# Opening: rests of k from ScalarE's queue and an earlier gate for GpSimd's loads; ending: a bank of its own for the last product and three queues for its stores

## The chip, the cores and the metric

One core of a Trainium2 chip. The metric is the device time of one execution in microseconds (us). "Fast" is the normal state of the runs; every comparison here is within that state, and every profile shown is of a fast run. The profiled span (from the first record to the last) is some 1.8 us shorter than the device time of the same run.

## The reference

A linear attention (phi(x) = elu(x) + 1) over 8 batches, 8 heads, 576 positions of 64, then a mixture of four dense experts:

```python
def phi(x): return np.where(x > 0, x, np.exp(x) - 1.0) + 1.0
kv  = np.einsum('bhsd,bhse->bhde', phi(k), v);  z = np.sum(phi(k), axis=2)
num = np.einsum('bhsd,bhde->bhse', phi(q), kv)
x   = num / (np.einsum('bhsd,bhd->bhs', phi(q), z)[..., None] + 1e-6)   # -> 4608 x 512
p   = domain_probs / (domain_probs.sum(-1, keepdims=True) + 1e-9)
for e in range(4):
    out += p[:, e:e+1] * (np.maximum(x @ w1[e], 0.0) @ w2[e])           # 512 -> 1024 -> 512
```

## The kernel before

The 576 positions of a batch are cut into 512 "first" ones and a "rest" of 64. A list of operations is ordered by a planner in the program: each operation has an engine, an estimated duration and a priority; GpSimd's order is the order in which the program adds its operations. Each layer's matrix product is done in seven half-size block products in place of eight. Four things matter here.

Loads. Every load is a DMA issued by a named queue. `hold` makes it wait for the landing of the load that carries the same `mark`:

```python
def load_first(queue, pri, t, pr, hold=None, mark=None):      # 256 KB: two heads, 512 positions
    ...
def load_first_rest(t, o, queue, pri, key, g):                # 32 KB: two heads, 64 positions
    n = 2 * R // DC
    dma(queue, pri, o[g * n : (g + 1) * n].rearrange("p h t d -> p h (t d)"),
        t[0, 2 * g : 2 * g + 2, NT:S].rearrange("h (p t) d -> p h (t d)", t=2),
        ((key, g),), 0.17)
```

The order of the first loads ("pair" is a pair of heads, counted from 0 to 3):

```python
load_first("SP", -9, k, 0, mark="k0")
load_first("SP", -8, q, 0)
load_first("SP", -7, k, 1)
for g in range(DC):
    load_first_rest(k, k_r, "ACT" if g < 2 else "SP", -6, "k_r", g)
for g in range(DC):
    load_first_rest(v, v_r32, "SP", -4, "v_r32", g)
load_first("SP", -3, q, 1)
load_first("POOL", 0, v, 0, hold="k0")          # GpSimd starts when k of pair 0 is in
for pr in (2, 3):
    load_first("POOL", 0, k, pr)
    load_first("POOL", 0, q, pr)
    if pr == 2:
        load_first("POOL", 0, v, 1)
        load_w1(0, (0,))                        # first quarter of the first w1, 128 x 1024
load_first("POOL", 0, v, 2)                     # eighth load of GpSimd
load_first("POOL", 0, v, 3)
```

The last products. P1 to P7 are the block products of layer two; a product is four matmuls into half of one of four PSUM banks:

```python
P4 = (2, 1, ...)        # bank 2, upper half
P3 = (2, 0, ...)        # bank 2, lower half: the last one
seq = (P1, P6, P5, P7, P4, P2, P3)              # in the very last unit
```

The six final adds on VectorE, and the four last stores (64 x 512 each, 128 KB):

```python
for dur, o, a_, b_, r, w in (
    (0.4,  of[:, 0],   hi(1), s15[:, 0], ...),
    (0.4,  of[:, 1],   hi(0), of[:, 0], ...),
    (0.62, of[:, 2:4], lo(3)[:, None].broadcast_to([P, 2, HD]), of[:, 0:2], ...),   # third
    (0.4,  of[:, 2],   hi(2), of[:, 2], ...),                                       # fourth
    (0.4,  of[:, 0],   lo(1), s15[:, 0], ...),
    (0.4,  of[:, 1],   lo(2), of[:, 1], ...),
):
    ...
    if i in (3, 5):
        for par, queue in enumerate(("SP", "ACT")):
            store(int(i == 3), par, queue, (O(2 if i == 3 else 0),))
```

Of the kernel before, what the change touches and what calls it, by code (L numbers as in the profile page):

```python
# [137 lines left out]
def kernel(  # L138
# [23 lines left out]
    HF = FC // 2  # L162
# [167 lines left out]
        dma(queue, pri, o, t[0, 2 * pr : 2 * pr + 2, 0:NT].rearrange("h (p c) d -> p h c d", c=C),  # L330
            (key,), 0.72, hold=hold, mark=mark)

    def load_first_rest(t, o, queue, pri, key, g):

        n = 2 * R // DC
        dma(queue, pri, o[g * n : (g + 1) * n].rearrange("p h t d -> p h (t d)"),
            t[0, 2 * g : 2 * g + 2, NT:S].rearrange("h (p t) d -> p h (t d)", t=2),
            ((key, g),), 0.17)

    def load_rest(b, queue, pri, after=0.0, parts=(0, 1, 2)):  # L340
        par = b % 2
# [636 lines left out]
    def l2_unit(n):  # L978
        j, s, e = units[n]
        h, s4 = h_b[n % 2], s4_b[n % 2]  # L980
        first, last = e == 0, e == E - 1
        H = lambda t, f: ("h", n % 2, t, f)
        Q = lambda i: ("s4", n % 2, i)
        KW = lambda i, j_: k2(e, i, j_)
        T = lambda i: (("t", e, i),)

        def prod(bank, half, a, w, opens):
            for c in range(HF):
                nc.tensor.matmul(  # L989
                    out=l2b[bank][:, half * HD : (half + 1) * HD],  # L990
                    lhsT=a[:, c, :],
                    rhs=w[:, c],
                    start=(opens and first and c == 0),
                    stop=(last and c == HF - 1),
                    skip_group_check=True,
                )

        P2 = (1, 0, h[:, 0, 1], H(0, 1), quad(e, 1, 0), KW(1, 0), True)
        P4 = (2, 1, h[:, 1, 1], H(1, 1), quad(e, 0, 1), KW(0, 1), True)
        P1 = (0, 0, h[:, 0, 0], H(0, 0), quad(e, 0, 0), KW(0, 0), True)  # L1000
        P5 = (0, 1, s4[:, 0], Q(0), t123[e][:, 0], T(0), False)
        P6 = (1, 1, s4[:, 1], Q(1), t123[e][:, 1], T(1), False)
        P7 = (3, 0, s4[:, 2], Q(2), t123[e][:, 2], T(2), True)
        P3 = (2, 0, s4[:, 3], Q(3), quad(e, 1, 1), KW(1, 1), False)
        seq = (P1, P4, P5, P2, P6, P7, P3)
        end = n == nu - 1
        if first:
            seq = (P1, P5, P2, P6, P7, P4, P3)
        elif end:
            seq = (P1, P6, P5, P7, P4, P2, P3)  # L1010
        p0 = U(n + 1) + 0.45
        for i, (bank, half, a, ak, w, wk, opens) in enumerate(seq):
            pl.add("PE", 0.436, p0 + 0.9 * i,
                   lambda bank=bank, half=half, a=a, w=w, opens=opens: prod(bank, half, a, w, opens),
                   r=(ak,) + wk, w=lk(bank) + ((("p", bank, half),) if end else ()))
        if not last:
            return
        oi = rot("ot", 2)
        ot = ot_b[oi]
        of = ot.rearrange("p a (b d) -> p (a b) d", b=2)  # L1020
        O = lambda i: ("ot", oi, i // 2)
        tt = nc.vector.tensor_tensor
        v2 = lambda bank: bank.rearrange("p (a d) -> p a d", a=2)
        s1, s5 = (s15[:, i : i + 1].broadcast_to([P, 2, HD]) for i in range(2))
        sk = ("s15", "ident", ("kvz", 2), ("kvz", 3))
        if end:
            pl.add("ACT", 0.36, p0, lambda: nc.scalar.copy(s15[:, 0], l2b[0][:, 0:HD]),
                   r=(("p", 0, 0),), w=sk)
        else:
            pl.add("ACT", 0.5, p0 + 3.5, lambda: nc.scalar.copy(  # L1030
                s15.rearrange("p a d -> p (a d)"), l2b[0]), r=("l2b0",), w=sk)
        stores = [(u, par) for u in range(2) for par in range(2)]

        def store(u, par, queue, r):
            b = 2 * (2 * s + u) + par
            dma(queue, p0 + 9, out[b * S + NT : (b + 1) * S, :],
                ot[par * R : (par + 1) * R, u, :], (), 0.3, r=r)

        if end:
            lo, hi = (lambda bank: l2b[bank][:, 0:HD]), (lambda bank: l2b[bank][:, HD : 2 * HD])  # L1040
            for dur, o, a_, b_, r, w in (
                (0.4, of[:, 0], hi(1), s15[:, 0], (("p", 1, 1), "s15"), (O(0),)),
                (0.4, of[:, 1], hi(0), of[:, 0], (("p", 0, 1),), (O(0),)),
                (0.62, of[:, 2:4], lo(3)[:, None].broadcast_to([P, 2, HD]), of[:, 0:2],
                 (("p", 3, 0), O(0)), (O(2),)),
                (0.4, of[:, 2], hi(2), of[:, 2], (("p", 2, 1),), (O(2),)),
                (0.4, of[:, 0], lo(1), s15[:, 0], ("l2b1",), (O(0),)),
                (0.4, of[:, 1], lo(2), of[:, 1], lk(2), (O(0),)),
            ):
                i = cnt.get("lp", 0)  # L1050
                cnt["lp"] = i + 1
                pl.add("DVE", dur, p0 + 2 + i * 0.5,
                       lambda o=o, a_=a_, b_=b_: tt(out=o, in0=a_, in1=b_, op=AO.add), r=r, w=w)  # L1053
                if i in (3, 5):
                    for par, queue in enumerate(("SP", "ACT")):
                        store(int(i == 3), par, queue, (O(2 if i == 3 else 0),))
            return
        pl.add("DVE", 0.62, p0 + 4.5, lambda: tt(
            out=of[:, 0:2], in0=v2(l2b[1]), in1=s1, op=AO.add), r=("l2b1", "s15"), w=(O(0),))
        pl.add("DVE", 0.4, p0 + 5.5, lambda: tt(  # L1060
            out=of[:, 2], in0=l2b[3][:, 0:HD], in1=of[:, 1], op=AO.add),
            r=("l2b3", O(0)), w=(O(2),))
        pl.add("DVE", 0.62, p0 + 6.5, lambda: tt(
            out=of[:, 1:4:2], in0=of[:, 1:3], in1=s5, op=AO.add), r=("s15",), w=(O(0), O(2)))
        pl.add("DVE", 0.62, p0 + 8, lambda: tt(
            out=of[:, 1:3], in0=v2(l2b[2]), in1=of[:, 1:3], op=AO.add), r=lk(2), w=(O(0), O(2)))
        r = (O(0), O(2))
        if j < NJ - 1:
            dma("SP", p0 + 9, out_t[j][:, 2 * s : 2 * s + 2, :], ot, (), 1.5, r=r)
        else:  # L1070
            for u, par in stores:
                store(u, par, "SP", r)


    def consts(i):
# [11 lines left out]
    nc.vector.memset(qTr[0], 0.0)  # L1087
    pl.add("DVE", 0.27, 36, lambda: nc.vector.memset(qTr[1], 0.0),
           w=[("qTr", 1, pr) for pr in range(DC)])
    load_first("SP", -9, k, 0, mark="k0")  # L1090
    load_first("SP", -8, q, 0)
    load_first("SP", -7, k, 1)
    for g in range(DC):
        load_first_rest(k, k_r, "ACT" if g < 2 else "SP", -6, "k_r", g)
    for g in range(DC):
        load_first_rest(v, v_r32, "SP", -4, "v_r32", g)
    load_first("SP", -3, q, 1)
    load_first("POOL", 0, v, 0, hold="k0")
    for pr in (2, 3):
        load_first("POOL", 0, k, pr)  # L1100
        load_first("POOL", 0, q, pr)
        if pr == 2:
            load_first("POOL", 0, v, 1)
            load_w1(0, (0,))
    load_first("POOL", 0, v, 2)
    load_first("POOL", 0, v, 3)
    first_rest()
# [121 lines left out]
```

## Time and profile before

| | before |
|---|---|
| device time, median (4 runs) | 496.66 us (496.15 to 497.3) |
| profiled span, granted clock | 494.7 us, 0.999 |
| v of pair 2 landed; its k-v product begins | 14.44; 14.48 |
| last product done; last add done | 489.07; 490.27 |
| last store landed; SyncE ready for the end barrier | 493.28; 493.73 |

The prediction below shows the slices, the stretches, the chain of waits and the end. To the views shown there, two lines on the very end are to be added: what SyncE waited for after 480 us (columns: who waits, for whom, us in total, number of waits, longest):

```profile
SPq L1224 <- DMA out_dram<-ot: 2.3, 2, 1.4
SPq L1224 <- PEq L1224: 0.9, 2, 0.7
```

L1224 is the end of the program. Each engine ends with a DRAIN and a barrier. SyncE waits for the stores to land, and after that 0.7 us at most for the others.

### The profile page before, as it was taken

The numbers are of one execution on the slowest core, as the hardware profiler recorded it, in microseconds if no ns is written. First come the engines' busy times: TensorE is split into PE (matmuls) and PEld (weight loads), VectorE is DVE, ScalarE is ACT, GpSimd is POOL, SyncE is SP. The second block draws the span as 40 slices with busy tenths as digits, with TensorE's granted clock in tenths as the row PEclk, the third lists the DMA queues.
The fourth block names the chain that finished last, engine by engine and source line by source line (L and its number), as shares of the span: only waits on it lengthen the run. The fifth ranks groups of instructions, "written<-read, shape, count | busy, mean of one in ns | idle before, by whom it ended". The sixth has DMA issues, their size and how long they took to land.

```text
span 494.7 us, 14994 instructions
## 1 busy us (share of the span) xinstructions
PE 484.2 (98%) x6092; PEld 429.3 (87%) x6092; DVE 413.0 (83%) x1045; ACT 364.8 (74%) x686; POOL 41.0 (8%) x66
## 2 busy tenths in 40 slices
PE   7999999999999999999999999999999999999995
PEld 5544547999999999999999999999999999999994
DVE  6798999999998989899988899899987676767664
ACT  5636678978977898769886997699766767676641
POOL 7656600000000000000000000000000000000000
PEclk9999999999999999999999999999999999999999
DMA  8999969956855674877557655655623232323311
GB/s 222 214 234 222 269 137 229 222 95 166 122 158 129 153 179 118 164 149 157 123 129 165 132 151 121 183 125 134 146 54 87 45 87 44 88 44 86 46 44 42
DMA packets 125541, 66.98 MB, mean 135 GB/s; under 512 B 94592, under 2 KB 119696, under 8 KB 125472
## 3 DMA queue, kind: packets, MB, share of 16 engines
q1 hardware_dynamic: 115808, 51.99, 46.8%
q0 software_dynamic: 9344, 13.71, 13.6%
q8 instruction: 47, 0.77, 0.6%
q10 hardware_dynamic: 320, 0.33, 0.2%
q14 instruction: 22, 0.18, 0.1%
HBM read 45.16 MB, written 9.44 MB: 110 GB/s over the span
## 4 chain that ended last, share of the span: by engine, by line
PE 91%; DVE 3%; DMA 3%; ACT 1%; POOL 1%; issue 1%; DVEq 0%; SPq 0%; ACTq 0%
PE l1b L913 40%; PE l2b L989 39%; PE l1b L750 4%; PE l2b L761 3%; PE at L653 2%; PE at L629 1%; DMA t<-in_v_dram 1%; DMA kqr<-in_k_dram 1%; DVE t L736 1%; DMA kq<-in_k_dram 1%; POOL w1x L290 1%; DVE w1x L715 1%; DVE ot L826 1%; PE l2b L750 0%; DVE ot L1053 0%
## 5 line engine op out<-in xcount | busy, mean ns | idle before, releaser
L913 PEld LDWEIGHTS <-w 128*128 128x128 f16 x2048 | 134.0, 98 | 5.3
L927 ACT ACTIVATE h<-l1b 128x512 f16<-128x512 f32 x128 | 76.7, 599 | 52.5 <-PE l1b L913 50.1
L989 PE MATMUL l2b<-w,h 128*128 128x256 f16 x768 | 115.0, 273 | 0.0
L989 PE MATMUL l2b<-t,s 128*128 128x256 f16 x768 | 114.5, 273 | 0.0
L913 PEld LDWEIGHTS <-w1x 128*128 128x128 f16 x1536 | 100.2, 98 | 4.2 <-issue 0.8
L989 PEld LDWEIGHTS <-s 128*128 128x128 f16 x1024 | 90.3, 98 | 6.2
L933 DVE CUSTOM_DVE_ANT_0 h<-l1b,p 128x512 f16<-128x512 f32 x64 | 44.1, 690 | 44.3 <-PE l1b L913 41.7
L913 PE MATMUL l1b<-xs,w1x 128*128 128x128 f16 x1024 | 78.1, 219 | 0.2 <-ACT l1b L930 0.2
L913 PE MATMUL l1b<-xs,w 128*128 128x128 f16 x1024 | 78.0, 219 | 0.0
L913 PE MATMUL l1b<-xT,w 128*128 128x128 f16 x1024 | 78.0, 219 | 0.0
L873 ACT ACTIVATE xp<-x,p_nat 128x512 f16<-128x512 f16 x112 | 77.3, 721 | 0.4
L989 PEld LDWEIGHTS <-h 128*128 128x128 f16 x768 | 67.3, 98 | 4.5
L975 DVE TENSOR_TENSOR s<-h 128x512 f16<-128x512 f16 x128 | 53.8, 420 | 2.1
L930 ACT COPY l1b<-l1b 128x512 f32<-128x512 f32 x64 | 36.8, 574 | 12.0 <-PE l1b L913 11.4
L930 ACT COPY u<-l1b 128x512 f32<-128x512 f32 x64 | 37.4, 585 | 10.8 <-PE l1b L913 10.4
L933 DVE CUSTOM_DVE_ANT_0 h<-l1b,u 128x512 f16<-128x512 f32 x64 | 43.8, 684 | 1.3 <-PE l1b L913 0.2
L930 ACT COPY p<-l1b 128x512 f32<-128x512 f32 x64 | 37.4, 584 | 8.6 <-PE l1b L913 7.6
L891 DVE TENSOR_TENSOR xs<-xT,xs 128x256 f16<-128x256 f16 x128 | 36.8, 288 | 3.5
L913 PE MATMUL l1b<-xT,w1x 128*128 128x128 f16 x512 | 39.0, 219 | 0.0
L989 PE MATMUL l2b<-w,s 128*128 128x256 f16 x256 | 38.4, 273 | 0.0
L594 ACT ACTIVATE ek<-kq 128x512 f16<-128x512 f32 x54 | 33.9, 629 | 2.4 <-DMA kq<-in_k_dram 1.7
L975 DVE TENSOR_TENSOR s<-s,h 128x512 f16<-128x512 f16 x64 | 27.1, 424 | 5.6
(155 smaller groups left out, 578.0 us busy)
## 6 DMA issues: line engine op xcount, KB each, us to landing
w<-in_moe_w_dram POOLq DMA_DIRECT2D x32, 256.0 KB, 8.0
out_dram<-ot SPq DMA_DIRECT2D x16, 512.0 KB, 3.0
kq<-in_k_dram SPq DMA_DIRECT2D x26, 256.0 KB, 3.3
kq<-in_q_dram SPq DMA_DIRECT2D x26, 256.0 KB, 3.2
vs<-in_v_dram SPq DMA_DIRECT2D x24, 256.0 KB, 3.5
xT<-xp SPq DMA_TRANSPOSE x64, 3.1
kq<-in_k_dram POOLq DMA_DIRECT2D x3, 256.0 KB, 7.2
vs<-in_v_dram POOLq DMA_DIRECT2D x3, 256.0 KB, 7.2
```

Source lines behind the costliest of these rows:

```text
L594: pl.add("ACT", 0.55, pri + i * step, lambda i=i: nc.scalar.activation(ek[:, i], kq[:, i], AF.Exp), r=(sk[i],), w=(("ek", ei, i),))
L653: nc.tensor.matmul(out=slot[c - c0], lhsT=qT[:, c] if c < C else qTr[par][:, pr], rhs=kvz, start=True, stop=True,)
L750: nc.tensor.matmul(out=bank[:, ts], lhsT=w1_sb[e][:, dc, fj * P : (fj + 1) * P], rhs=xt0[:, dc, ts], start=(dc == 0), stop=(dc == DC - 1 a ...
L761: nc.tensor.matmul(out=bank, lhsT=hts[ht[fj]][:, c * P : (c + 1) * P], rhs=w2_sb[e][:, fj, :], start=(fj == 0), stop=(fj == FC - 1),)
L873: pl.add("ACT", 0.6, pri, lambda c=c, src=src, ps=ps: nc.scalar.activation(xp[:, c, :], src, AF.Copy, scale=ps), r=r, w=(("xp", xi, c),))
L891: lambda o=o, a=a, b_=b_: tt(out=o, in0=a, in1=b_, op=AO.subtract),
L913: nc.tensor.matmul(out=bank[:, fc * P : (fc + 1) * P], lhsT=wt[:, kc, fc * P : (fc + 1) * P], rhs=r[:, kc, :], start=(start and fc == 0 an ...
L927: return lambda: nc.scalar.activation(o, bank, AF.Relu)
L930: return lambda: nc.scalar.copy(o, bank)
L933: return lambda: nc.vector._custom_dve(TENSOR_ADD_SAT, out=o, in0=bank, in1=t, s0=BIG, s1=0.0)
L975: pl.add("DVE", 0.36, U(n + 1) + d - 0.5, lambda i=i, a=a, b_=b_, alu=alu: tt(out=s4[:, i], in0=a, in1=b_, op=alu), r=r, w=(Q(i),))
L989: nc.tensor.matmul(out=l2b[bank][:, half * HD : (half + 1) * HD], lhsT=a[:, c, :], rhs=w[:, c], start=(opens and first and c == 0), stop=( ...
```

## The change

Its intent: GpSimd's loads start earlier, because their gate is a 32 KB load that lands before k of pair 0; the small loads leave SyncE's queue so that q of pair 1 is issued early; the loads of GpSimd that TensorE needs last come last. At the end the last product gets a PSUM bank that nothing else reads, so that the add of bank 2 needn't wait for it, and the last four stores go out on three queues.

```diff
-    def load_first_rest(t, o, queue, pri, key, g):
+    def load_first_rest(t, o, queue, pri, key, g, mark=None):
 ...
-            ((key, g),), 0.17)
+            ((key, g),), 0.17, mark=mark)
 ...
+        free = cnt["l1u"][0]
+        end = n == nu - 1
+
         def prod(bank, half, a, w, opens):
+            own = end and (bank, half) == (2, 0)
+            out_ = l1b[free][:, 0:HD] if own else l2b[bank][:, half * HD : (half + 1) * HD]
 ...
-                    start=(opens and first and c == 0),
-                    stop=(last and c == HF - 1),
+                    start=(((opens and first) or own) and c == 0),
+                    stop=((last or n == nu - 2) and c == HF - 1),
 ...
-                (0.4, of[:, 2], hi(2), of[:, 2], (("p", 2, 1),), (O(2),)),
+                (0.62, of[:, 1:3], v2(l2b[2]), of[:, 1:3], (("p", 2, 1),), (O(0), O(2))),
                 (0.4, of[:, 0], lo(1), s15[:, 0], ("l2b1",), (O(0),)),
-                (0.4, of[:, 1], lo(2), of[:, 1], lk(2), (O(0),)),
+                (0.4, of[:, 1], l1b[free][:, 0:HD], of[:, 1], ("l1b%d" % free,), (O(0),)),
 ...
-                    for par, queue in enumerate(("SP", "ACT")):
+                    for par, queue in enumerate(("SP", "POOL" if i == 3 else "ACT")):
 ...
-    load_first("SP", -9, k, 0, mark="k0")
-    load_first("SP", -8, q, 0)
-    load_first("SP", -7, k, 1)
+    for pr in range(2):
+        load_first("SP", -9 + pr, k, pr)
+        load_first("SP", -9 + pr, q, pr)
     for g in range(DC):
-        load_first_rest(k, k_r, "ACT" if g < 2 else "SP", -6, "k_r", g)
+        load_first_rest(k, k_r, "ACT", -9, "k_r", g, mark=None if g else "go")
     for g in range(DC):
         load_first_rest(v, v_r32, "SP", -4, "v_r32", g)
-    load_first("SP", -3, q, 1)
-    load_first("POOL", 0, v, 0, hold="k0")
+    load_first("POOL", 0, v, 0, hold="go")
     for pr in (2, 3):
         load_first("POOL", 0, k, pr)
         load_first("POOL", 0, q, pr)
-        if pr == 2:
-            load_first("POOL", 0, v, 1)
-            load_w1(0, (0,))
+    load_first("POOL", 0, v, 1)
+    load_w1(0, (0,))
     load_first("POOL", 0, v, 2)
     load_first("POOL", 0, v, 3)
```

More of the change, by code (lines that the diff above doesn't have):

```diff
@@ L985, in l2_unit @@
         T = lambda i: (("t", e, i),)
+        free = cnt["l1u"][0]
+        end = n == nu - 1
         def prod(bank, half, a, w, opens):
+            own = end and (bank, half) == (2, 0)
+            out_ = l1b[free][:, 0:HD] if own else l2b[bank][:, half * HD : (half + 1) * HD]
             for c in range(HF):
                 nc.tensor.matmul(
-                    out=l2b[bank][:, half * HD : (half + 1) * HD],
+                    out=out_,
                     lhsT=a[:, c, :],
                     rhs=w[:, c],
-                    start=(opens and first and c == 0),
-                    stop=(last and c == HF - 1),
+                    start=(((opens and first) or own) and c == 0),
+                    stop=((last or n == nu - 2) and c == HF - 1),
                     skip_group_check=True,
@@ L1005, in l2_unit @@
         seq = (P1, P4, P5, P2, P6, P7, P3)
-        end = n == nu - 1
         if first:
@@ L1014, in l2_unit @@
                    lambda bank=bank, half=half, a=a, w=w, opens=opens: prod(bank, half, a, w, opens),
-                   r=(ak,) + wk, w=lk(bank) + ((("p", bank, half),) if end else ()))
+                   r=(ak,) + wk,
+                   w=(("l1b%d" % free,) if end and i == 6 else lk(bank)) + ((("p", bank, half),) if end else ()))
         if not last:
```

## The prediction

> **What bounds the kernel now.** I read four views, from coarse to fine. First the page's slices, 12.4 us each:
>
> ```profile
> PE   7999999999999999999999999999999999999995
> DVE  6798999999998989899988899899987676767664
> PEclk9999999999999999999999999999999999999999
> DMA  8999969956855674877557655655623232323311
> ```
>
> TensorE (PE) is nine tenths busy or more in every slice but the first and the last, at a full granted clock. Nothing that lies between those slices can pay unless it takes work from TensorE, and the change takes none. So the second view is the busy time by stretch; its columns are the stretch, then its length, PE, PE's weight loads, DVE, ACT and POOL busy with their instruction counts, then clock, DMA share and GB/s:
>
> ```profile
> 10.00:14.50 4.50, 2.97 (x39) 2.04 (x38) 4.12 (x14) 3.66 (x10) 3.97 (x7) 1.00 1.20 253
> 14.50:20.00 5.50, 5.05 (x57) 3.31 (x57) 3.96 (x13) 3.63 (x10) 3.70 (x6) 1.00 1.14 203
> 100.00:200.00 100.00, 100.00 (x1379) 95.11 (x1378) 91.39 (x238) 83.64 (x159) 0.00 (x0) 1.00 0.63 141
> 484.00:494.70 10.70, 5.05 (x55) 4.38 (x52) 5.46 (x12) 0.97 (x2) 0.00 (x0) 0.97 0.16 49
> ```
>
> TensorE has gaps before 14.5 us, loses about half a microsecond between 14.5 and 20, and none between 100 and 200. (Before 14.5 much of what it does is keep-warm matmuls, so even its busy time there is not progress.) After that the kernel is a fixed amount of TensorE work that slides as a block. Its start is set in the opening, its end is followed by some 5.7 us of tail. The third view is the chain of waits in the opening (start, length, what):
>
> ```profile
> 0.74 3.17 DMA kq<-in_k_dram
> 3.91 0.30 issue
> 4.21 0.84 POOL w1x L290
> ...
> 9.20 5.24 DMA t<-in_v_dram
> 14.44 0.04 issue
> 14.48 0.71 PE l2b L504 x12
> ```
>
> The first load of k lands at 3.91; only then may GpSimd issue, one load after another, from 4.21; its eighth load (v of head pair 2) is issued at 9.20, lands at 14.44, and releases the k-v product of pair 2, the last wait of TensorE for memory on this chain. Later TensorE stops once more, 0.45 us at 19.25 for ScalarE's copy of pair 2's transposed x. The fourth view is the same opening's DMA, by microsecond:
>
> ```profile
> 3.00:4.00 1.00, 1.00 (x7) 0.69 (x5) 0.82 (x4) 0.07 (x1) 0.00 (x0) 1.00 1.06 362
> 5.00:6.00 1.00, 1.00 (x7) 0.69 (x6) 0.90 (x4) 0.64 (x2) 1.00 (x3) 1.00 0.71 121
> 6.00:7.00 1.00, 1.00 (x13) 0.91 (x12) 0.78 (x3) 0.72 (x2) 1.00 (x2) 1.00 0.98 129
> 8.00:9.00 1.00, 1.00 (x17) 0.85 (x16) 0.00 (x0) 0.13 (x1) 1.00 (x2) 1.00 1.02 354
> ```
>
> There is a hole from 5 to 7 us: about 125 GB/s where 354 to 362 flow beside it. SyncE's early loads are through and GpSimd's have not arrived. From 7 us on the DMA share stays at or above one until some 60 us. The end, in the chain of waits and in the timeline:
>
> ```profile
> 488.39 0.70 DVE ot L1053
> ...
> 489.19 0.42 DVE ot L1053
> 489.61 0.33 DVEq L1224
> 489.94 0.33 DVE ot L1053
> ```
> ```profile
> 488.46 0.60 PE L989 MATMUL l2b<-w,s 128*128 128x256 f16 x4
> 489.64 1.13 SPq L290 DMA_DIRECT2D out_dram<-ot  x2
> 489.64 1.38 ACTq L290 DMA_DIRECT2D out_dram<-ot  x2
> ```
>
> The last product is done at 488.46 + 0.60 = 489.06. VectorE runs its six final adds nearly without a pause from 487.40 to 490.27. The fourth add starts at 489.19, 0.10 after the third ends (489.09); the second-to-third gap is as long (488.29 to 488.39), so that is the cost of one add needing the one before it.
>
> **What the Trainium skill says.** "DMA: Bandwidth & Descriptors", section "Issuing engines are not separate DMA queues": loads from SyncE, ScalarE and GpSimd share the same 16 engines, so another issuer saves only issue time. The trace agrees: from 7 us the share is at one whoever issues. Its "Specifications" put the memory's limit for one core at about 358 GB/s; the trace peaks at 354 to 362. "PSUM — Partial Sum Buffer", section "PSUM bank collisions raise a hardware error", tells to guard a bank as a whole and not by address; the built program does that, and the listing of its waits shows the fourth add waiting for all of bank 2, the last product included. "Perfetto Trace Analysis", section "Optimizing Scalar/DVE Operations", gives VectorE about 125 ns of fixed cost for an operand in PSUM. The final adds fit: 0.42 us for 128x256 and 0.70 for 128x512, so 0.28 per 256 columns and 0.14 fixed.
>
> **The change, part by part.** (1) GpSimd's gate. It now waits for the first 32 KB rest of k, issued at 0.74 on ScalarE's queue, not for the 256 KB k at 3.91. The two rests that ScalarE issued before took a median 2.6 us to land and the fastest small load of that tile took 2.4, so the first lands at 3.15 to 3.35. With the same 0.30 of wake-up GpSimd starts at 3.45 to 3.65: 0.55 to 0.75 earlier. (2) GpSimd's order. k and q of pairs 2 and 3 come before v of pair 1 and the first w1. The same seven loads stand ahead of v of pair 2, so it keeps the eighth place, 4.99 us after the first issue. If it still needs 5.24 us it lands 0.65 earlier, near 13.8. The hole can pay for that: two microseconds at 125 in place of 355 GB/s are 460 KB, or 1.3 us of transfer at the peak. Moved back are v of pair 1 (fourth to sixth) and the first w1 (fifth to seventh). In before, v of pair 1 was used at 11.06; two 256 KB loads at the 0.73 us spacing of GpSimd's issues cost it 1.5 us and the early start returns 0.65: about 11.9. The first w1, estimated from the same spacing, lands near 13.2, still before 13.8. (3) All rests of k on ScalarE: four issues of 0.46 instead of two, so its activation-table load starts at about 2.6 instead of 1.69 and, at 1.28 us, ends at 3.87; its first exponential ran at 3.93. Free, with 0.05 to spare. SyncE loses two issues, and q of pair 1 moves from 5.13 to about 2.3. (4) The instruction order that follows: VectorE and ScalarE do phi of pairs 2 and 3 before the normalisation of pair 1. VectorE has less left after 14.5 us. I credit 0.15, a third of the 0.45 stop at 19.25. Opening in sum: -0.65 - 0.15 = -0.8.
>
> (5) The end. The last product goes to a free bank, so the fourth add need not wait for it; as shown, it was held equally by the third add. Its price is that both halves of bank 2 are now added in the fourth add, 128x512 at 0.70 in place of 128x256 at 0.42: +0.28 on a chain that VectorE alone sets. (6) The stores. The first pair goes out from SyncE and GpSimd, the second from SyncE and ScalarE. In before, ScalarE's second issue began at about 490.3, when the last add ended (490.27), so the busy queue hid nothing; I credit at most 0.05. A store issued by GpSimd is slower to start, but leaves 0.6 us ahead of the last pair. End in sum: +0.3. TensorE's instructions in the middle are as many as before; some six keep-warm matmuls disappear. Net: -0.8 + 0.3 = -0.5 us on 496.7, or 496.2.
>
> **The rivals.** First, the opening gains nothing: the DMA stream is the limit, and the loads of GpSimd merely slow q of pair 0 and k and q of pair 1, or TensorE, whose order is fixed, stops at v of pair 1. For it speaks the share of 1.06 at 3 to 4 us; against it the hole just after. Then only the end's +0.3 is left: 497.0. Second, the opening gains more: TensorE's stop at 19.25 goes entirely and the hole is filled: -1.3, with the end 495.7. Third, the end really waited for the last product by a little that the modelled end of matmuls hides, and the first stores profit from a queue of their own: end 0 to -0.2, total 495.8. Fourth, the store from GpSimd lands last: GpSimd's loads needed 4.0 us at the median when the engines were loaded; issued at 489.95 this would be 493.95, against about 493.4 for the other pair. That costs 0.5 more, total 496.7. Fifth, the new order in the middle opens or closes a small TensorE gap (70 to 80 us has 0.21 idle): 0.2 either way.
>
> **Range and chances.** The opening's size (0 to 1.3) carries a doubt of about 0.4, the end's of 0.25, and the median of three runs, whose spread was 1.15 us in before, of 0.4: together some 0.6. So 496.2, with 495.3 to 496.9 to hold it 8 times in 10. Two per cent are 9.9 us. Even all of the time before 14.5 us and the tail's 5.7 could not give or take this without a breakdown: within 2% 0.98, faster 0.01, slower 0.01.
>
> **What would show it.** Right: GpSimd's first issue at 3.5 to 3.7; v of pair 2 landed near 13.8 and TensorE's k-v product there; the block of TensorE work from 30 us on 0.6 to 1.0 earlier; the fourth final add 0.70 long, and 0.25 to 0.3 more between the last matmul and the last add. Wrong: v of pair 2 landing at 14.3 or later, or TensorE idle before the product of pair 1 and not catching up; the last add ending no later after the last matmul than the 1.2 us of before (490.27 against 489.06); or GpSimd's store as the last to land.

## The result, and the profile after

The changed kernel took 498.22 us at the median of four runs (497.92 to 498.9), against 496.66 before. The ratio is 1.0033, 95% interval 1.0015 to 1.005. (A ratio here is the mean time of one kernel's fast runs over the mean of the other's fast runs of the same rounds, so not quite the ratio of the medians.) That is 1.6 us slower where half a microsecond faster was predicted, and outside the predicted range.

The middle is as it was. The page's slices of after:

```profile
PE   7999999999999999999999999999999999999993
PEclk9999999999999999999999999999999999999998
DMA  8999968966655575768567755656632222342411
```

By stretch (columns as in the prediction: length, PE, weight loads, DVE, ACT, POOL, clock, DMA share, GB/s), and the two microseconds in which before had its hole:

```profile
10.00:14.50 4.50, 2.76 (x37) 2.13 (x35) 3.97 (x14) 3.94 (x10) 3.30 (x6) 1.00 1.21 191
14.50:20.00 5.50, 5.46 (x61) 3.59 (x61) 3.18 (x11) 2.96 (x8) 3.75 (x7) 1.00 1.17 207
484.00:496.60 12.60, 4.74 (x51) 4.07 (x48) 5.41 (x12) 0.97 (x2) 0.55 (x1) 0.89 0.15 42
```
```profile
5.00:6.00 1.00, 1.00 (x8) 0.73 (x7) 0.86 (x3) 0.49 (x1) 1.00 (x3) 1.00 1.15 329
6.00:7.00 1.00, 1.00 (x13) 0.92 (x12) 0.68 (x2) 0.63 (x1) 1.00 (x2) 1.00 1.34 256
```

TensorE is busy for 5.46 of the 5.50 us from 14.5 to 20 (5.05 before): its stop at 19.25 is gone. The hole is filled, 329 and 256 GB/s for 121 and 129. The last stretch, though, is 12.6 us long in place of 10.7, and GpSimd now does something in it. The chain of waits in the opening:

```profile
3.49 0.84 POOL w1x L290
...
8.40 6.08 DMA t<-in_v_dram
14.48 0.04 issue
14.53 0.71 PE l2b L504 x12
```

GpSimd starts at 3.49 for 4.21 and issues v of pair 2 at 8.40 for 9.20, as predicted. But in this execution the load took 6.08 us in place of 5.24, and the k-v product begins at 14.53 for 14.48. The end, in the timeline (start, length, engine, line, what, count, idle before it and its releaser):

```profile
488.13 0.60 PE L994 MATMUL l1b<-w,s 128*128 128x256 f16 x4
488.42 1.49 DVE L1058 TENSOR_TENSOR ot<-l2b,ot 128x512 f32<-128x512 f32 x2 [0.46 <-PE l2b L994]
...
490.20 0.55 POOL L290 DMA_DIRECT2D out_dram<-ot  x1 [427.16 <-DVE ot L1058]
490.60 0.55 ACTq L290 DMA_DIRECT2D out_dram<-ot  x1
```

The last product is done at 488.13 + 0.60, 488.74 unrounded: 0.32 earlier than before. VectorE's third add starts at 488.42 after 0.46 idle; before there was no such pause. GpSimd's store is its first instruction in 427 us. And the chain of waits, followed back from the end, has changed its nature:

```profile
62.77 427.41 issue
490.18 0.57 POOLq L1227
```

Where before it led from the last store through the final adds into TensorE's work, it now ends on GpSimd's sequencer at the end of the program (L1227) and goes back from there to GpSimd's last load at 62 us. The waits of SyncE say the same from the other side:

```profile
SPq L1227 <- PEq L1227: 2.3, 2, 1.8
```

After the stores have landed, SyncE waits 1.8 us (0.7 before) for the end barrier. "PEq" is only the engine that passes the barrier on. The timeline does not list DRAINs, but the view of the last line does (shortest, median and longest in ns, first and last start in us), here before and after:

```profile
L1224 POOLq DRAIN  x3: 51/102/8427, 61.6 to 494.2; - x3
L1227 POOLq DRAIN  x3: 51/102/5625, 490.2 to 496.3; - x3
```

The long one is GpSimd's. From the trace's records (us from the start of the span):

```
                  GpSimd's last DMA issue   its DRAIN          SyncE ready   end of span
before            62.39 (ends)              61.65 to  70.07    493.73        494.71
after             490.75 (ends)             490.18 to 495.80   494.22        496.60
```

GpSimd's DRAIN ends 5.05 us after its store was issued, although that store had landed at 493.21, before ScalarE's (493.70). In before the same DRAIN ran at 61 to 70 us, where nobody waited for it. It is no fixed 5.6 us: over the eighteen traces it ended at the later of two times, within 0.1 us, namely 2.5 us after the landing of GpSimd's last DMA (2.49 to 2.53 in fifteen kernels, before among them) and 5.05 us after the end of its issue (after, and the two kernels below with one store moved to GpSimd). SyncE, by contrast, was ready 0.45 to 0.52 us after the last landing. So the span, 1.88 us longer, falls into these parts (each the difference of two event times in the two traces):

| part | after less before, us |
|---|---|
| TensorE's block (last product done 489.07 -> 488.74) | -0.32 |
| last product to end of last add (1.21 -> 1.83) | +0.62 |
| last add to last landing (3.01 -> 3.13) | +0.12 |
| landing to SyncE ready (0.45 -> 0.52) | +0.07 |
| SyncE ready to end of GpSimd's DRAIN | +1.58 |
| from there to the end of the span (0.98 -> 0.79) | -0.19 |
| sum | +1.88 |

### The profile page after: what moved, and what is told of

It is laid out like the page before. It is cut to its first block, busy times and chain, and to the rows that moved or that the text cites. A ratio compares the mean times of both kernels' runs of the same rounds, so it can differ in the third digit from the quotient of the medians.

```text
span 496.6 us, 14996 instructions
## 1 busy us (share of the span) xinstructions
PE 483.8 (97%) x6089; PEld 429.1 (86%) x6089; DVE 413.1 (83%) x1045; ACT 364.9 (73%) x686; POOL 41.4 (8%) x67
## 4 chain that ended last, share of the span: by engine, by line
issue 87%; DMA 5%; DVE 3%; POOL 2%; PE 1%; ACT 0%; POOLq 0%; DVEq 0%
DMA w<-in_moe_w_dram 3%; DMA t<-in_v_dram 1%; DVE t L736 1%; DVE w1x L715 1%; POOL w1x L290 1%; DVE h L785 1%; DMA t<-in_k_dram 0%; DVE ot L826 0%; PE l1b L750 0%; POOL w L290 0%; POOL xp L290 0%; PE l2b L750 0%; PE l2b L504 0%; POOL prawr L290 0%; ACT h L788 0%
```

## The experiments

Theory: GpSimd's late store costs 1.6 us through its DRAIN; the opening is worth what was predicted and hidden by noise; the final adds cost a little more than predicted. Rivals: the opening is worth nothing; any store on a third queue costs; the bank costs. Sixteen kernels ran in four batches; ratios are against the kernel before in the same batch, five rounds each. (In the expectations e1 is the opening alone, e3 the change with its store back, e13 and e14 the opening alone with four memsets and with one.)

### The opening alone, with before's end

```diff
+    for pr in range(2):
+        load_first("SP", -9 + pr, k, pr)
+        load_first("SP", -9 + pr, q, pr)
+        load_first_rest(k, k_r, "ACT", -9, "k_r", g, mark=None if g else "go")
+    load_first("POOL", 0, v, 0, hold="go")
 ... (before with the change's whole hunk of loads; products, adds and stores as before)
```

> The opening of the change with the end of the kernel before. My theory: the loss is all at the end, and the opening is worth a little: the profile of the changed kernel had its TensorE block 0.32 to 0.39 us earlier, so this runs 0.2 to 0.5 us under the kernel before (about 496.3 against 496.7), and no GpSimd drain stands at the end. Rival (the new opening itself costs time, through the shares of the loads that lag): 0.3 us or more above the kernel before.

Measured: 496.29 us, ratio 0.9984 (0.9971 to 0.9997). In its chain of waits:

```profile
8.45 5.20 DMA t<-in_v_dram
13.65 0.04 issue
13.70 0.71 PE l2b L504 x12
```

Issued at nearly the same time as in after (8.45 for 8.40), v of pair 2 takes 5.20 here and lands 0.8 earlier than in before. The opening by itself pays about 0.8 us (interval 0.15 to 1.4), more than the 0.2 to 0.5 expected. TensorE's first layer-two product starts 1.21 earlier, 0.43 more than the k-v product's 0.78, because the stop at 19.25 is gone here too.

### The end alone, with before's opening

```diff
-    load_first("POOL", 0, v, 0, hold="go")
+    load_first("POOL", 0, v, 0, hold="k0")
 ... (after with before's whole hunk of loads; products, adds and stores as after)
```

> The end of the change with the opening of the kernel before. My theory: 1.9 to 2.4 us above the kernel before: 1.6 for GpSimd's drain, 0.28 for the wider fourth add, and up to 0.34 for the late start of the third add. Rival (the end is neutral as the prediction nearly said): at most 0.4 us above.

Measured: 499.01 us, ratio 1.0044 (1.003 to 1.0058). GpSimd's DRAIN runs from 490.59 to 496.45, SyncE was ready at 494.99. The whole loss, and more, is in the end. Here the third add was not late: from the last product to the last add 1.48 us, 0.27 over before, which is the wider fourth add (0.70 for 0.42).

### The change with GpSimd's store back on ScalarE

```diff
-                    for par, queue in enumerate(("SP", "POOL" if i == 3 else "ACT")):
+                    for par, queue in enumerate(("SP", "ACT")):
```

> The changed kernel with one word put back: the second store of the first pair goes out from ScalarE's queue again, not from GpSimd's. My theory: GpSimd's drain at the end of the program shrinks to nothing, and the time falls by about 1.6 us against the changed kernel, to 496.4 to 496.8, level with the kernel before. Rival (the cost is in the adds and the extra bank): it falls by less than 0.5 us.

Measured: 497.07 us, ratio 1.0004 (0.9991 to 1.0017). One word of the program takes the ratio from 1.0033 to 1.0004. GpSimd's DRAIN is back at 61.51 to 69.93. That the time is not below before, although the opening pays, has two reasons in its profile: v of pair 2 landed at 14.83, and from the last product to the last add it is 1.83 us, as in after.

### Before with only that store on GpSimd

```diff
-                    for par, queue in enumerate(("SP", "ACT")):
+                    for par, queue in enumerate(("SP", "POOL" if i == 3 else "ACT")):
```

> The kernel before with one word changed: the second store of the first pair from GpSimd's queue. My theory: GpSimd's drain runs for about 5 us after that store's issue and ends 1.5 to 1.9 us after SyncE is ready; the kernel is 1.3 to 1.9 us slower than the kernel before. Rival (only the store's own landing matters): the other pair still lands last and it is within 0.3 us.

Measured: 498.75 us, ratio 1.0038 (1.0025 to 1.0051): the store costs 1.9 us in a kernel that has nothing else of the change. SyncE's wait at the end, to be held against the 0.9, 2, 0.7 of before:

```profile
SPq L1224 <- PEq L1224: 2.5, 2, 1.8
```

### A store of GpSimd 26 us before the end

One of the four rest stores of the tile before the last, from GpSimd instead of SyncE:

```diff
-                store(u, par, "SP", r)
+                store(u, par, "SP" if par == 0 or u else "POOL", r)
```

> Before, with one of the four rest stores of the tile before the last (about 26 us before the end) issued by GpSimd instead of SyncE; everything else as before. Theory (only a store that GpSimd issues in the last few us costs, because its drain at the end of its program runs some 5 us after the store's issue and holds the end barrier): GpSimd's drain ends near 475 us, hidden, and the time is within 0.3 us of before, 496.7 to 497.2. Rival (any store from GpSimd late in the program costs, for instance because GpSimd must sit in a long wait or its queue is slower to shut down): 1.6 us or more over before, 498.5.

Measured: 496.91 us, ratio 0.9998 (0.9983 to 1.0012). GpSimd's DRAIN runs from 471.62 to 477.25, 5.63 us as in after and in the kernel above (5.62 in both), and SyncE's wait for the barrier is that of before (0.9 us in two, 0.7 at most).

So it isn't GpSimd's store as such that costs, nor its 400 us of sleep before it, but the DRAIN that follows when it has no time left to hide in.

### The three parts of the opening, one at a time

The gate alone:

```diff
-        load_first_rest(k, k_r, "ACT" if g < 2 else "SP", -6, "k_r", g)
+        load_first_rest(k, k_r, "ACT" if g < 2 else "SP", -6, "k_r", g, mark=None if g else "go")
-    load_first("POOL", 0, v, 0, hold="k0")
+    load_first("POOL", 0, v, 0, hold="go")
```

> Before, with only the gate of GpSimd's loads moved from the first load of k to the first rest of k on ScalarE's queue. Theory (gate is worth 0.55 to 0.75 us on v of pair 2, which is the load that TensorE waits for at 14.4 us): GpSimd's first issue near 3.5 us instead of 4.2, v of pair 2 issued near 8.5 instead of 9.2, time 0.4 to 0.8 us below before, noise of 0.4 from the slowest share. Rival (the load order and the rests do the gain): no change, within 0.2.

Measured: 497.95 us, ratio 1.0024 (1.0011 to 1.0037): slower, against both expectations. The first 16th of v of pair 2 landed at 13.34, as in before (13.37): no gain at all, although GpSimd started earlier. In this profile's chain of waits TensorE's second pair hangs on q of pair 1, which SyncE still issues tenth:

```profile
5.14 5.67 DMA kq<-in_q_dram
```

It lands at 10.81; in before it landed at 8.63. GpSimd's 256 KB loads probably stand in front of it now. That is not the whole loss: the k-v product of pair 2 begins at 14.63, only 0.15 later than in before. Where the rest of the 1.2 us goes is open.

The order of GpSimd's loads alone:

```diff
-        if pr == 2:
-            load_first("POOL", 0, v, 1)
-            load_w1(0, (0,))
+    load_first("POOL", 0, v, 1)
+    load_w1(0, (0,))
     load_first("POOL", 0, v, 2)
```

> Before, with only the order of GpSimd's loads changed (v of the second pair and the first slab of w1 behind k and q of the fourth pair instead of ahead of them). Theory: v of pair 2 stays the eighth load of GpSimd, issued near 9.2 us, so no gain at 14.4 us; the time is within 0.3 us of before. Rival (k and q of pair 3 two loads earlier free ScalarE and VectorE and so TensorE): 0.5 us or more faster.

Measured: 497.17 us, ratio 1.0023 (1.0 to 1.0046). Without the earlier start, v of pair 1, two places further back, landed at 13.70, and TensorE, whose order is fixed, stood waiting for it until 13.74 (11.12 in before). The ratio rests on two of the six runs, 499.61 and 500.05 us at lower granted clocks (0.995 and 0.990); the other four took 496.78 to 497.43.

The rests alone (all on ScalarE, q of pair 1 early, the gate on k of pair 0):

```diff
+    for pr in range(2):
+        load_first("SP", -9 + pr, k, pr, mark=None if pr else "go")
+        load_first("SP", -9 + pr, q, pr)
-        load_first_rest(k, k_r, "ACT" if g < 2 else "SP", -6, "k_r", g)
+        load_first_rest(k, k_r, "ACT", -9, "k_r", g, mark=None)
-    load_first("SP", -3, q, 1)
```

> Before, with only the rests of k all on ScalarE's queue and q of the second pair early on SyncE's queue; the gate stays on the first load of k and GpSimd's order stays. Theory: GpSimd issues at the same times as before, v of pair 2 is issued near 9.2; the stretch 3 to 9 us moves the same bytes, so within 0.3 us of before. Rival (the order of the small loads frees VectorE in the opening): 0.4 us or more faster.

Measured: 498.19 us, ratio 1.0034 (1.0019 to 1.0049), slower. The hole at 5 to 6 us is filled (332 GB/s), but GpSimd starts as late as before, and v of pair 2 comes as late (13.69 to 14.53). The first layer-two product starts 1.66 later than in before. TensorE's stop for ScalarE's copy of x, now at 20.3 us, is 0.45 as in before and explains none of it. The clock can: in this profile it was granted at half from 15.55 to 18.97 us, 0.69 over the stretch (third number from the end; before's is 1.00):

```profile
14.50:20.00 5.50, 5.43 (x47) 3.58 (x47) 2.38 (x7) 3.09 (x9) 3.65 (x6) 0.69 1.16 208
```

3.42 us at half clock are an estimated 1.7 us of TensorE's work. What lowered the clock is not shown; TensorE had just stood idle for 1.61 us before v of pair 2. Nor is it all: the two of the five runs with the highest mean clocks (0.997 and 0.999) took 498.19 and 498.27, so the loss of this kernel stays without a shown cause.

### The three pairs of parts

Each is the opening alone with one part put back to before. Gate and rests, without the order:

```diff
+        if pr == 2:
+            load_first("POOL", 0, v, 1)
+            load_w1(0, (0,))
-    load_first("POOL", 0, v, 1)
-    load_w1(0, (0,))
```

> Before with two of the three parts of the opening: the gate on the first rest of k, and the rests of k on ScalarE's queue with q of the second pair early; the order of GpSimd's loads stays as before. Theory (the earlier gate only pays when q of the second pair no longer waits behind nine issues of SyncE, where it landed at 10.8 us with the gate alone; the order of GpSimd's loads adds little): v of pair 2 is the eighth load as in e1, so the time is within 0.3 us of e1: ratio 0.998 to 0.999. Rival (the order is needed as well): no faster than before, ratio 1.000 or above.

Measured: 496.55 us, ratio 1.0002 (0.9985 to 1.002). The interval holds both expectations.

Gate and order, without the rests:

```diff
-    for pr in range(2):
-        load_first("SP", -9 + pr, k, pr)
-        load_first("SP", -9 + pr, q, pr)
+    load_first("SP", -9, k, 0, mark="k0")
+    load_first("SP", -8, q, 0)
+    load_first("SP", -7, k, 1)
-        load_first_rest(k, k_r, "ACT", -9, "k_r", g, mark=None if g else "go")
+        load_first_rest(k, k_r, "ACT" if g < 2 else "SP", -6, "k_r", g, mark=None if g else "go")
+    load_first("SP", -3, q, 1)
```

> Before with the gate and the order of GpSimd's loads, the rests of k and q of the second pair as before. Theory: q of the second pair lands near 10.8 us as with the gate alone, and TensorE's second pair starts near 12.5 us or later; no gain, ratio 1.000 to 1.003. Rival (the rests do nothing): as e1, 0.998.

Measured: 497.62 us, ratio 1.0019 (1.0007 to 1.0031). In its profile q of pair 1 landed at 11.77 and the k-v product of pair 1 began at 13.93 (11.12 in before), as in the expectation and later; v of pair 1 had landed at 13.10.

Rests and order, without the gate:

```diff
-        load_first("SP", -9 + pr, k, pr)
+        load_first("SP", -9 + pr, k, pr, mark=None if pr else "go")
-        load_first_rest(k, k_r, "ACT", -9, "k_r", g, mark=None if g else "go")
+        load_first_rest(k, k_r, "ACT", -9, "k_r", g, mark=None)
```

> Before with the rests of k on ScalarE's queue, q of the second pair early, and the order of GpSimd's loads, but the gate left on the first load of k. Theory: GpSimd starts 0.7 us later than in e1, near 4.2, and every load behind it lands as much later, so v of pair 2 is near 14.4; ratio 0.999 to 1.002, 0.4 to 0.8 us over e1. Rival (the gate does nothing): as e1, 0.998.

Measured: 499.26 us, ratio 1.0046 (1.0028 to 1.0063); more than expected. The profiled run's mean granted clock was 0.990, and the trace says where it was low:

```profile
14.50:20.00 5.50, 5.50 (x48) 4.23 (x46) 2.48 (x9) 2.60 (x7) 3.48 (x6) 0.50 1.17 208
```

The clock was at half from 13.25 to 20.08 us; the drop falls into a wait of TensorE, 1.18 us for v of pair 1. 6.83 us at half clock are an estimated 3.4 us of its work; its last product ends 3.19 later than in before. Four of the six runs are alike (mean clock 0.990 to 0.992, 498.9 to 500.14 us), the two at 0.997 took 497.13 and 497.77. So most of the 0.46% is probably clock, and the two other runs are 0.4 to 1.1 over before.

What tells the parts apart is the landing of v of pair 2, from the trace's records, in its sixteen shares (one per DMA engine). The first shows when its turn came, the last releases TensorE:

| opening | profiles | first share, us | last share, us |
|---|---|---|---|
| before's | 4 | 13.26 to 13.79, mean 13.45 | 14.44 to 14.98, mean 14.64 |
| gate | 1 | 13.34 | 14.58 |
| order | 1 | 13.67 | 15.63 |
| rests | 1 | 13.69 | 14.53 |
| gate + order | 1 | 13.62 | 15.04 |
| rests + order | 1 | 13.52 | 15.47 |
| gate + rests | 1 | 12.54 | 14.06 |
| all three | 7 | 12.59 to 13.33, mean 12.75 | 13.64 to 15.13, mean 14.20 |

Only gate and rests together bring the turn forward, by 0.7 us (not in one of the seven, at 13.33). The gate gives GpSimd an earlier start; the rests fill the hole, for from 5 to 6 us the profiles with them show 313 to 344 GB/s and those without 121 to 143, gate or not. That either alone only changes the order of the same bytes is my reading and not tested further. The order then decides what TensorE's plan does with it; its own worth (0.9984 against 1.0002) is within the two intervals and stays open.

The last column shows why one profile could not tell this: the last share trails the first by 0.84 to 2.15 us, and with the same opening it came at 13.64 or at 15.13.

### v of pairs 2 and 3 ahead of the first w1

```diff
     load_first("POOL", 0, v, 1)
-    load_w1(0, (0,))
     load_first("POOL", 0, v, 2)
     load_first("POOL", 0, v, 3)
+    load_w1(0, (0,))
```

> The new opening with the end of before (as e1), and the two v loads of the third and fourth pair put ahead of the first slab of w1 on GpSimd's queue. Theory (the landing of v of pair 2 sets the opening, and it lands when the bytes ahead of it have passed): it is issued 0.55 earlier and half a megabyte fewer lie ahead of it, so it lands 0.5 to 1.2 us earlier than in e1 (13.65), and the time falls to 495.3 to 496.0. Rival (the slab of w1 then comes last and TensorE waits for it instead): TensorE's first layer-one product moves to 14.5 or later and the time stays at 496.3 or above.

Measured: 497.34 us, ratio 1.0004 (0.9985 to 1.0024): no gain, the rival. v of pair 2 landed at 13.37, 0.28 earlier than with the opening alone, less than expected; its k-v product began at 14.30, the first layer-one product only at 16.16 (14.34 with the opening alone), released by the slab of w1 that came last (issued at 9.90, landed 6.21 later).

### Each pair of last stores as one

```diff
-                    for par, queue in enumerate(("SP", "ACT")):
-                        store(int(i == 3), par, queue, (O(2 if i == 3 else 0),))
+                    u = int(i == 3)
+                    b0 = 2 * (2 * s + u)
+                    dma("ACT" if u else "SP", p0 + 9,
+                        out.rearrange("(b t) d -> b t d", t=S)[b0 : b0 + 2, NT:S, :],
+                        ot[:, u, :], (), 0.6, r=(O(2 if u else 0),))
```

> As e1, with each last pair of stores (two of 64 partitions on two queues) as one store of 128 partitions: the first half from ScalarE, the second from SyncE. Theory (the end waits for the last landing, and fewer descriptors and one queue less do not lengthen it): 0.0 to 0.3 us below e1, 496.0 to 496.3. Rival (one queue takes longer than two for the same bytes): the last store lands over 3.3 us after the last add instead of 3.0, 496.6.

Measured: 506.03 us, ratio 1.0179 (1.0160 to 1.0198): nine microseconds slower, which neither theory had. By stretch, this kernel at the end, and then the opening alone (two stores per half) in its two microseconds of storing:

```profile
496.00:498.00 2.00, 0.00 (x0) 0.00 (x0) 0.00 (x0) 0.00 (x0) 0.00 (x0) 0.50 0.13 51
```
```profile
490.00:491.00 1.00, 0.00 (x0) 0.00 (x0) 0.00 (x0) 0.00 (x0) 0.00 (x0) 1.00 0.96 260
```

A DMA share of 0.13 is two of sixteen engines, at 51 GB/s, for about ten microseconds. The outermost dimension of the store's target is 2 (two batches, whose rests aren't adjacent). The Trainium skill has the rule: "DMA: Bandwidth & Descriptors", section "Rules for kernel authors", says under "Use all 16 engines" that an outermost dimension under 16 confines the whole DMA to at most so many engines. The trace agrees.

### The late third add: its place in VectorE's stream

Of VectorE's six last adds the third starts 0.45 us after the second ends in after, and 0.10 after it in before, though both semaphores that it waits for had come: the product P7's at 487.44 and the second add's own at 487.98, with the start at 488.42 (after's records). I looked through VectorE's records in all the kernels for pauses over 0.3 us in which no semaphore changed shortly before the end. There are few; I found them at records number 575, 703, 959 and 1343 of VectorE's stream. The third add is number 1343 in after and with the opening alone, and number 1336 in before. Two kernels shift it, each being the opening alone with memsets of 128x1 in the middle of the run:

```diff
+                if n == nu - 24 and i == 0:
+                    for x in range(4):                 # or range(1)
+                        nc.vector.memset(pad[:, x : x + 1], 0.0)
                 tt(out=s4[:, i], in0=a, in1=b_, op=alu)
```

> As e1, with four memsets of 128x1 on VectorE put in near the middle of the run, before one add of the layer-two sums, so that all VectorE instructions after it lie four places later in its stream. Theory (the third of the last adds starts 0.35 late because it is the record with number 1343 of VectorE's stream, 63 over a multiple of 64, as is the one other stall in before that no semaphore explains, number 959, and the stream is refilled there): the third add becomes number 1347 and starts within 0.1 us of the add before it, 0.35 us earlier relative to the last product; the time is 0.3 us below e1, 495.9 to 496.1. Rival (a semaphore or the bank of the product delays it): the third add still starts 0.12 us after the end of the product before the last, 0.40 after the add before it, and the time is that of e1.

Measured: 496.87 us, ratio 0.9985 (0.9969 to 1.0002). The third add is number 1347 and starts 0.11 us after the second: on time. The time isn't below the opening alone; the spread of its six runs (495.5 to 498.16) is far over the 0.35 in question, and in its profile v of pair 2 landed at 15.13. The pause, not the time, is what this pair of kernels can decide.

> Control to e13: as e1, with one such memset instead of four. Theory of the place in the stream: number 1343 is now the semaphore wait just ahead of the third add, so the third add is as late as in e1 (0.3 to 0.5 us after the end of the add before it), and the time is that of e1, 496.3. Rival (any change of VectorE's stream, or the memset's effect on time, removes the lateness): the third add is on time here too.

Measured: 496.08 us, ratio 0.9980 (0.9967 to 0.9993). The third add, now number 1344, starts 0.10 after the second. In its timeline the second to fourth adds run as one group without a pause (x3; with the opening alone the pause of 0.46 parts them):

```profile
487.58 1.75 DVE L1059 TENSOR_TENSOR ot<-l2b,ot 128x256 f32<-128x256 f32 x3
```

The control did not do what the theory had it do: the wait just ahead of the third add, then number 1343, did not stall. These two runs alone would also fit the rival that any memset removes the lateness. The eighteen traces settle it. Take every instruction from record 190 on that comes directly after a semaphore wait while VectorE is idle. Where its number is 63 over a multiple of 128 it starts 0.39 to 0.47 us after the wait: 36 cases, at 447, 575, 959, 1087, 1215 and 1343, without an exception. At any other number it starts at most 0.18 after it: 2850 cases. In the control, number 1343 was the wait itself and not the instruction behind one.

In four kernels, before among them, number 1343 is VectorE's DRAIN in the end barrier, and that is late too (0.44 to 0.47 us after its wait). From SyncE ready to the end of the span it takes 0.98 us in before and 0.75 to 0.77 in the kernels where no late DRAIN holds the end: this is behind the -0.19 in the table of parts. The third add over the 18 kernels traced:

| third add is number | kernels | starts after the second add's end | last product to last add |
|---|---|---|---|
| 1343 | 5 (after, the opening alone, the change with its store back, whole stores, rests + order) | 0.45 to 0.47 | 1.57 to 1.83 |
| 1336 to 1338, 1344, 1345, 1347 | 13 | 0.10 to 0.11 | 1.21 to 1.49 |

The Trainium skill has a candidate for the cause: "Runtime: NRT & Kernel Launch", section "Instruction fetch mechanics", tells of an instruction memory that is refilled in blocks, 256 instructions to 16 KiB (so 64 bytes each), and calls the cost at a boundary mostly hidden. The trace lists packets of 8 KB of kind "instruction" on queue q14 (and of 16 KB on q8); at that size, by estimate, 8 KB are 128 instructions, the period of the late places. "Mostly hidden" fits too, as most multiples show no pause. But the refill is argued here, not shown: no run forced one, and for the third add of the opening alone the nearest such packet begins 0.68 us after the late start, so it isn't what that start waited for. Shown are the place, and that shifting the stream by one or by four places takes the 0.35 us away.

### The whole change, mended

```diff
-                    for par, queue in enumerate(("SP", "POOL" if i == 3 else "ACT")):
+                    for par, queue in enumerate(("SP", "ACT")):
 ...
+                if n == nu - 24 and i == 0:
+                    for x in range(1):
+                        nc.vector.memset(pad[:, x : x + 1], 0.0)
```

> The whole change with its two faults taken out: the store of GpSimd goes back to ScalarE's queue (as e3), and one memset of 128x1 in VectorE's stream moves the third add off record number 1343 (as e14). Theory: the third add starts within 0.1 us of the add before it, from the last product to the end of the last add is 1.48 us (1.83 less 0.35), 0.28 more than in before for the wider fourth add; the time is 0.35 below e3 and 0.3 above e14: ratio 0.999. Rival (the wider fourth add and the bank cost or gain more than their own duration): ratio at or over 1.000, or at or under 0.998.

Measured: 495.92 us, ratio 0.9993 (0.9981 to 1.0006). From the last product to the last add 1.49 us, 0.28 over before's 1.21: exactly the wider fourth add.

The opening alone with one memset has the lowest ratio of all: 0.9980 of before, with an interval that ends below one (0.9993); the opening alone, at 0.9984, ends below one too, and after is 1.0033. They were not run in one batch.

## Why the prediction was wrong

**The failed step is (6), with the fourth rival.** It said of the GpSimd store: "slower to start, but leaves 0.6 us ahead of the last pair", credited 0.05, and the rival "the store from GpSimd lands last" gave it 0.5 more. It counted only the landing. The landing was no trouble (493.21, ahead of ScalarE's 493.70). What it left out is that GpSimd ends its program with a DRAIN, that this DRAIN still runs for 2.5 us or more after its last DMA has landed (2.59 in after), and that the end barrier waits for all engines. In after it came 1.58 us behind SyncE. The store alone cost 1.9 us, a store of the same size 26 us earlier nothing, and taking it out of the change 1.4 us (1.0033 to 1.0004). The view that would have told was at hand: in before's records GpSimd's DRAIN lasts until 7.7 us after its last DMA issue, hidden at 61 to 70 us. "A queue that has been silent for 400 us is free" was the thought; it is not free to finish.

**Step (5), the adds: right in its size, short by a term.** The fourth add took 0.69 to 0.70 as said, and in the mended kernel and in the end alone the add's 0.27 to 0.28 is all there is. The bank of its own brought nothing, as said: the third add held the fourth anyway. In after, 0.35 came on top, from the third add's place in VectorE's stream. No reading of the diff could have given that; the number of instructions ahead of it changed by seven.

**Steps (1) and (2), the gate and the order: right in the times of issue, optimistic on the landing.** The hole of 5 to 7 us is one in bytes: in its second half the DMA share was 0.98, and the gate alone leaves its first half at 143 GB/s; the rests fill it. Start at 3.49 (predicted 3.45 to 3.65), v of pair 2 issued at 8.40. Its turn came 0.70 earlier over seven profiles, but its last share only 0.44 (14.64 to 14.20), with 1.5 us of scatter; in after's own profile it came at 14.48, which the prediction named as a sign that it was wrong. The reasoning credited the gain to the gate; the runs gave it to the gate and the rests together.

**Step (4): too low.** It credited 0.15 for the stop at 19.25; in after and in the opening alone practically all of it went (0.44 and 0.43 between the k-v product and the first layer-two product). So the sum of the opening, -0.8, came out right (0.9984 is -0.8 us) by luck, from two terms that were off in opposite directions: about -0.44 and -0.43. (Places in VectorE's stream are in the 0.9984 too: 0.35 lost at the third add, 0.22 won at the end barrier.)

**Step (3)** held: ScalarE's four issues cost nothing that a run showed.

**Two readings of the skill.** The 358 GB/s are no ceiling of this trace, which has 372 GB/s from 34 to 36 us in before. That VectorE's 0.14 us fits the page's 125 ns is not established: "Perfetto Trace Analysis", section "Optimizing Scalar/DVE Operations", adds that profiled durations are about twice its figure, and 0.14 comes from profiled durations. Nothing in the sum rests on either.

**The sum:** predicted -0.8 + 0.3 = -0.5; in the profile of after -0.32 (this execution's opening) + 0.62 + 0.19 (landing) + 1.58 - 0.19 = +1.88.

**The chances** (within 2%) held. The range did not hold, because all its rivals varied the parts that were on the list, and the cost was on none.

## What to carry to other kernels

Before a late DMA moves to an engine whose own program ended long ago, look at what that engine does at the end of its program; the end waits for the slowest engine's shutdown, not only for the last byte. An opening's parts can be worth nothing one by one and something together, so judge a reorder of loads by the time at which the load in question gets its turn (its first share), over several profiles, and not by one landing. Look at the granted clock stretch by stretch before you explain a slow opening: two profiles here ran 3.4 and 6.8 us of it at half clock. Where a chain of small instructions ends the kernel, check for pauses that no semaphore explains, and try whether shifting the stream by one instruction moves them.

## What the Trainium skill lacked or had wrong

- "DMA: Bandwidth & Descriptors", section "Issuing engines are not separate DMA queues", says that the issuer only matters for issue time. No page that I found says what a DMA from GpSimd costs at the end of the program: GpSimd's DRAIN was 5.62 to 5.63 us long after a 128 KB store in three kernels (5.87 in a fourth) and 8.4 us after its loads in before, in fifteen of eighteen kernels until 2.5 us after its last DMA had landed, and held the end by 1.46 to 1.58 us when the store was the last thing it did.
- The same page, section "Rules for kernel authors", advises one transfer of 128 partitions in place of two of half the partitions. Taken without the row on 16 engines, it cost 9 us here: the target's outermost dimension was 2, and 256 KB went through two engines at 51 GB/s. The two rows should name each other.
- "Runtime: NRT & Kernel Launch", section "Instruction fetch mechanics", calls the cost at a block's boundary mostly hidden. Here VectorE loses 0.39 to 0.47 us wherever the instruction after a semaphore wait has a number 63 over a multiple of 128 (36 of 36 cases). The page gives 16 KiB blocks; the trace of the opening alone has 47 instruction packets of 16 KB on one queue and 29 of 8 KB on another. Whether the pause is the refill is not shown.
- No page gives a figure for the spread of one load's sixteen shares under load: for the same 256 KB load it was 0.84 to 2.15 us from first to last, and the consumer waits for the last.
